# More unread products between TensorE's first steps, in banks chosen by another rule

## The chip, the cores and the metric

The kernel runs on one core of a Trainium2 chip. The metric is device time in microseconds (us) of one execution. Three executions of the kernel before gave 292.33, 293.51 and 296.66 us; a fourth, profiled one gave 292.35 us, and every duration below comes from that one.

## What is computed

Attention with an exponential feature map and no softmax matrix, and behind it a feed-forward layer with a maximum over three products:

```
def phi(x):
    proj = einsum('bhsd,df->bhsf', x, w_phi)
    proj = proj - max(abs(proj), axis=-1)
    return concatenate([exp(proj), exp(-proj)], axis=-1)
q_p, k_p = phi(q), phi(k)
kv  = einsum('bhsf,bhsd->bhfd', k_p, v)
z   = sum(k_p, axis=2)
att = einsum('bhsf,bhfd->bhsd', q_p, kv) / (einsum('bhsf,bhf->bhs', q_p, z) + 1e-6)
x   = att, heads side by side            # 4608 x 512
h   = maximum(maximum(x @ w1, x @ w2), x @ w3)
out = h @ w_out                          # 4608 x 512
```

There are 8 batches of 8 heads, 576 tokens a head, head size 64, 128 features, and a hidden width of 768. Inputs and output are float32; TensorE multiplies bfloat16.

## The kernel before

**Units and chunks.** The attention is cut into 16 units of four heads of one batch, two units a batch. The feed-forward layer is cut into chunks of 512 tokens, one a batch and one for the tokens that are left over. Both are described as nodes: a node is one step on one engine, with its instructions, the buffers it uses and the nodes it depends on.

**One unit** (`attention`, L428) loads q, k and v; casts q and k to bfloat16; transposes them (`tps`, L491, on TensorE for the first four units, else by DMA) and copies the result to `qkT` (L494, VectorE); projects them with w_phi (`psq`, `psk`, L528 and L533); takes maxima on VectorE (L552, `mqp` for q, `mk` for k) and exponentials of the k projection on ScalarE (`Ek`, L546); scales v on GpSimd by an exponential of the k maxima (`em`, L584, and `vab`, L588); computes the transposed q projection less its maximum (`psm`, L615 and L618 in the first four units) and its exponentials on ScalarE (`Eq`, L626); then forms kv (`kvps`, L642), the numerator and denominator (`psn`, L660) and their quotient (`x_sb`, L667). Among the steps of the first two units stand steps that prepare weights: transposes `pwT` (L800) and products `pm` (L814).

**Order.** Nothing is scheduled while the kernel runs. A table of words (`PLAN`, L97) gives every node an engine, a planned start in us, and the number of each buffer slot that it takes. A node `13T1@5.9` is node 13 on TensorE (T), with slot 1, at 5.9 us; D, A, G and S stand for VectorE, ScalarE, GpSimd and SyncE. `plan` (L250) reads the table. Each engine runs its instructions in the order of planned starts and waits on semaphores for what it needs.

**Banks.** TensorE writes into eight banks of 2 KB a partition. Each result takes a bank by number. When a new tile is made in a bank, its first writer waits for the last user of the tile that was there, and that includes an earlier write of TensorE itself.

**Unread products.** `fill` (L268) goes through TensorE's nodes in planned order. Where the plan leaves a gap between the end of one and the start of the next, it puts in products that nobody reads: 128x512, of a constant tile `idle`, made at L846 (tile `idler`). They go in at steps of 0.43 us up to 4.6 us of the plan (`SLOW`) and of 0.26 us from there on; gaps of up to 0.35 us are left alone up to `WARM` = 28 us of the plan, and of up to 0.5 us behind it. For each it looks for a bank in which no result lies around that time: the planned use of every result in it has ended by 0.1 us before, or begins over 0.6 us after. A product that is put in is itself recorded in `spans`, as a use of 0.5 us.

The names that the prediction speaks of are the products (L846), the first transposes (L491), the projections (L528, L533), `psm` (L615, L618), `pwT` (L800) and `kvps` (L642). In the diff the changed loop is L281 to L287.

Of the kernel before, what the change touches and what calls it, by code (L numbers as in the profile page):

```python
# [41 lines left out]
X_PE = 6  # L42
SUBT = 4
HALVES = 1
WARM = 28.0
SLOW = 4.6
JOIN = 2
MOVE = 5
# [219 lines left out]
def fill(order, spare, make, ready):  # L268

    pool = spare.pool  # L270
    spans, todo, free = {}, [(n.start, n.fn) for n in order], 0.0
    for n in order:
        for b in n.bufs:
            if b.pool is pool and b is not spare:
                x = spans.setdefault(id(b), [b.index, n.start, n.end])
                x[1], x[2] = min(x[1], n.start), max(x[2], n.end)
    for n in order:
        if n.eng != "PE":
            continue
        gap, t = n.start - free, max(free + 0.1, ready)  # L280
        while gap > (0.35 if t < WARM else 0.5) and t < n.start - 0.2:  # L281
            for i in range(len(pool.last)):
                if all(x[0] != i or x[2] < t - 0.1 or x[1] > t + 0.6 for x in spans.values()):
                    todo.append((t, make(i)))
                    spans[t] = [i, t, t + 0.5]
                    break
            t += 0.26 if t > SLOW else 0.43  # L287
        free = n.start + n.costs["PE"]
    return [fn for _, fn in sorted(todo, key=lambda x: x[0])]

# [2 lines left out]
def kernel(  # L293
# [554 lines left out]
    for fn in fill(order, spare, product, n_idle.end):  # L848
        fn()
# [28 lines left out]
```

## Time and profile before

| what | value |
|---|---|
| median of three executions | 293.51 us (292.33 to 296.66) |
| the profiled execution | 292.35 us |
| its span in the trace | 290.6 us |
| TensorE matmul busy | 279.4 us, 96% |
| VectorE, ScalarE, GpSimd busy | 215.9, 189.9, 117.4 us |
| unread products (L846) | 23, from 1.0 to 16.8 us |
| their length, shortest, median, longest | 0.376, 0.634, 0.634 us |
| last work of TensorE ends | 285.9 us |

How to read the views: busy times are what an engine spent in its instructions. A matmul's end is modelled and matmuls overlap, so a TensorE that reads as busy is not at its peak, and the start times tell more than the busy time. In a timeline, columns are start, length, engine, line, operation, written tile and what it was made from, shape and count; in square brackets stands the idle time ahead of it and what ended it. A line with a count is a run of instructions that follow each other, and its length reaches from the first start to the last end. The chain of waits follows the work that ended last back through what released each step.

### The profile page before, as it was taken

The page shows a single profiled execution, that of the slowest core. Times are in us where ns is not written, and L with a number is a line of the kernel's source. Part 1 is how long each engine was busy: PE and PEld are TensorE (multiplying, and loading weights), DVE is VectorE, ACT ScalarE, POOL GpSimd, SP SyncE. Part 2 cuts the span into 40 slices and gives each one's busy share as a digit, 9 for nine tenths or more (in the row PEclk, how much of TensorE's full clock was granted, in tenths as well). Part 3 has the DMA queues.
Part 4 walks back from the last instruction along what each step waited for, and adds up shares of the span by engine and source line. Part 5 has one row for each costly group of instructions (what it writes and reads, how often), then busy time and mean ns, then how long its engine had stood idle before and what let it go on. Part 6 is the DMA issues. An engine that isn't in the chain of part 4 may idle for free.

```text
span 290.6 us, 8659 instructions
## 1 busy us (share of the span) xinstructions
PE 279.4 (96%) x3602; PEld 158.7 (55%) x3641; DVE 215.9 (74%) x457; ACT 189.9 (65%) x438; POOL 117.4 (40%) x101
## 2 busy tenths in 40 slices
PE   8878999999999999999999999999999999999993
PEld 3556685646645585564466556545555564444442
DVE  2987999998876899768989959898796583242360
ACT  1599798977988899799669797566858631120101
POOL 8086886276093751552780519107064300000000
PEclk9999999999999999999999999999999999999999
DMA  7999988997967799796995779658534523500605
GB/s 191 208 201 181 218 249 271 230 335 178 356 132 258 221 189 279 165 287 130 298 182 106 173 235 206 138 126 174 102 107 95 112 21 72 126 18 2 144 18 128
DMA packets 63051, 49.87 MB, mean 172 GB/s; under 512 B 43556, under 2 KB 48036, under 8 KB 63012
## 3 DMA queue, kind: packets, MB, share of 16 engines
q1 hardware_dynamic: 58644, 44.04, 61.2%
q0 software_dynamic: 4288, 5.21, 11.0%
q8 instruction: 28, 0.46, 0.6%
q14 instruction: 11, 0.09, 0.1%
q10 hardware_dynamic: 80, 0.07, 0.1%
HBM read 34.67 MB, written 9.44 MB: 152 GB/s over the span
## 4 chain that ended last, share of the span: by engine, by line
PE 86%; DVE 6%; ACT 4%; DMA 2%; issue 1%; SPq 0%; ACTq 0%
PE ups L713 30%; PE ops L746 16%; PE ops L741 11%; PE kvps L642 7%; PE psn L660 6%; PE psq L533 5%; PE psm L613 4%; DVE mqp L552 2%; DMA wphi_f<-in_w_phi_dram 2%; DVE mk L552 2%; ACT Ek L546 2%; PE tps L491 1%; PE pxT L680 1%; PE psm L618 1%; PE psq L528 1%
## 5 line engine op out<-in xcount | busy, mean ns | idle before, releaser
L588 POOL TENSOR_TENSOR vab<-v_raw,em 128x1152 bf16<-128x1152 f32 (+1 forms) x36 | 68.2, 1907 | 88.7 <-ACT em L584 67.7
L713 PE MATMUL ups<-xT,w_bf 128*128 128x512 bf16 x411 | 100.7, 379 | 1.1
L546 ACT ACTIVATE Ek<-psk 128x512 bf16<-128x512 f32 x128 | 70.5, 607 | 23.7 <-PE psk L533 17.0
L626 ACT ACTIVATE Eq<-psm 128x512 bf16<-128x512 f32 (+1 forms) x160 | 79.2, 586 | 7.9 <-PE psm L613 6.2
L713 PEld LDWEIGHTS <-w_bf 128*128 128x128 bf16 x432 | 40.3, 98 | 44.1 <-DVE x_sb L667 0.2
L746 PE MATMUL ops<-wout_bf,hT 128*128 128x512 bf16 (+1 forms) x219 | 50.7, 373 | 0.3
L552 DVE TENSOR_REDUCE mqp<-psq 128x4 bf16<-128x512 f32 (+1 forms) x80 | 47.7, 631 | 2.0 <-PE psk L533 1.0
L719 DVE TENSOR_TENSOR hT<-hT,ups 128x512 bf16<-128x512 bf16 x54 | 35.9, 683 | 14.2 <-ACT hT L721 6.8
L552 DVE TENSOR_REDUCE mk<-psk 128x4 f32<-128x512 f32 x64 | 42.5, 681 | 1.7 <-ACT Ek L546 1.2
L746 PEld LDWEIGHTS <-hT 128*128 128x128 bf16 x222 | 21.3, 98 | 22.8 <-DVE hT L719 0.2
L721 ACT ACTIVATE hT<-ups 128x512 bf16<-128x512 f32 x28 | 16.4, 613 | 26.2 <-PE ups L713 26.1
L667 DVE TENSOR_TENSOR x_sb<-psn,rden 128x320 bf16<-128x320 f32 x64 | 31.5, 492 | 2.2
L660 PEld LDWEIGHTS <-Eq 128*128 128x128 bf16 x640 | 24.5, 97 | 6.5 <-issue 0.3
L754 DVE COPY osb<-ops 128x512 f32<-128x512 f32 (+1 forms) x19 | 12.6, 674 | 18.9 <-PE ops L746 18.9
L660 PE MATMUL psn<-kv_sb,Eq 128*128 128x65 bf16 x640 | 26.3, 193 | 0.1
L723 DVE TENSOR_SCALAR hT<-ups 128x512 bf16<-128x512 f32 x26 | 17.5, 686 | 11.4 <-PE ups L713 11.1
L754 ACT COPY osb<-ops 128x512 f32<-128x512 f32 (+1 forms) x18 | 10.3, 575 | 23.7 <-DMA out_dram<-osb 9.6
L741 PE MATMUL ops<-xT 128*128 128x512 bf16 x86 | 24.1, 380 | 0.5
L642 PEld LDWEIGHTS <-Ek 64*128 64x128 bf16 x1152 | 18.4, 94 | 5.7 <-issue 2.8
L642 PE MATMUL kvps<-vab,Ek 64*128 64x65 bf16 x1152 | 20.5, 190 | 0.9 <-POOL vab L588 0.5
L533 PE MATMUL psq<-w,qkT 64*128 64x128 bf16 x256 | 20.4, 217 | 0.4 <-DVE qkT L494 0.4
L533 PEld LDWEIGHTS <-qkT 64*128 64x128 bf16 x512 | 14.5, 94 | 10.7 <-issue 7.7
(72 smaller groups left out, 277.8 us busy)
## 6 DMA issues: line engine op xcount, KB each, us to landing
v_raw<-in_v_dram SPq DMA_DIRECT2D x16, 576.0 KB, 4.6
out_dram<-osb SPq DMA_DIRECT2D x70, 128.0 KB, 2.4
k_raw<-in_k_dram SPq DMA_DIRECT2D x12, 576.0 KB, 4.9
q_raw<-in_q_dram SPq DMA_DIRECT2D x12, 576.0 KB, 6.1
w_bf<-in_moe_w_dram POOLq DMA_DIRECT2D x3, 768.0 KB, 10.0
qk_bf<-in_q_dram POOLq DMA_DIRECT2D x3, 288.0 KB, 10.6
qk_bf<-in_k_dram POOLq DMA_DIRECT2D x3, 288.0 KB, 11.1
wout_bf<-in_moe_w_out_dram POOLq DMA_DIRECT2D x1, 768.0 KB, 9.5
```

The lines of the kernel that those rows point to most:

```text
L533: nc.tensor.matmul(ps()[:, i, :], lhsT=cols[r, :], rhs=w2[r, c, :], start=True, stop=True)
L546: nc.scalar.activation(Ek[s]()[:, tiles_of(t0, n), :], of(1), EXP, scale=1.0 - 2.0 * s)
L552: nc.vector.tensor_reduce((mq, mk)[c]()[:, tiles_of(t0, n)], of(c), AXX, ALU.max, apply_absolute_value=True)
L588: (nc.vector if n_.eng == "DVE" else nc.gpsimd).tensor_tensor(vab()[:, g, t0:t1, 0:D], vb()[:, t0:t1, :], em()[:, g, t0:t1].unsqueeze(2).t ...
L626: nc.scalar.activation(Eqb()[s][:, cols], psm()[:, 0:w], EXP, scale=1.0 - 2.0 * s)
L642: nc.tensor.matmul(kvps[ab]()[:, t // NT, g, :], lhsT=Ek[g]()[r, t, :], rhs=vab()[r, g, t, :], start=(t + g == 0), stop=(t == UT - 1 and g ...
L660: nc.tensor.matmul(psn()[:, c, :], lhsT=Eqb()[g][:, t0:t0 + P], rhs=kv()[:, pr, ab, g, :], start=(g == 0), stop=(g == 1))
L667: nc.vector.tensor_tensor(x_sb()[:, pr, :, ab, :], psn()[:, :, 0:D], rden().to_broadcast([P, 5, D]), ALU.mult)
L713: nc.tensor.matmul(ups(), lhsT=w_bf[i + 1][:, ct, j * P:(j + 1) * P], rhs=tokens_of(ct), start=(ct == 0), stop=(ct == CT - 1))
L719: nc.vector.tensor_tensor(hT()[:, j, :], hT()[:, j, :], ups(), ALU.max)
L741: nc.tensor.matmul(ops_()[:, 0:width], lhsT=tile_of(ct, tt), rhs=line_w[c_i > MOVE][:, ct, cols], start=(ct == 0), stop=False)
L746: nc.tensor.matmul(ops_()[:, 0:width], lhsT=hT()[:, j, tt * P:(tt + 1) * P], rhs=wout_bf[:, j, cols], start=False, stop=(j == JT - 1))
```

## The change

`WARM` goes from 28 to 34, and the loop of `fill` is changed in these ways:

- up to `WARM`, gaps from 0.25 us on get products (before: 0.35);
- products go in up to 0.1 us ahead of the waiting step (before: 0.2), 0.22 us apart (before: 0.26);
- where the gap is over 0.6 us, up to two more go in right ahead of the waiting step (`late`);
- a bank may also be taken if its next planned use begins with the waiting step or later (before: over 0.6 us after the product);
- a product is no longer recorded in `spans`, so a bank that one product took is free for the next, and the search, which goes from bank 0 up, takes the first that fits each time.

The table of the order is the same, and so are all other steps. In the built program there are 49 products where there were 23. 38 of them wait for TensorE's own count of the product directly ahead of them; before, the nearest such wait was for the last but one.

```diff
-WARM = 28.0
+WARM = 34.0
...
         gap, t = n.start - free, max(free + 0.1, ready)
-        while gap > (0.35 if t < WARM else 0.5) and t < n.start - 0.2:
+
+        late = 2 if gap > 0.6 and t < WARM else 0
+        while gap > (0.25 if t < WARM else 0.5) and (t < n.start - 0.1 or late):
+            if t >= n.start - 0.1:
+                t, late = n.start - 0.02 * late, late - 1
             for i in range(len(pool.last)):
-                if all(x[0] != i or x[2] < t - 0.1 or x[1] > t + 0.6 for x in spans.values()):
+                if all(x[0] != i or x[2] < t - 0.1 or x[1] >= n.start for x in spans.values()):
                     todo.append((t, make(i)))
-                    spans[t] = [i, t, t + 0.5]
                     break
-            t += 0.26 if t > SLOW else 0.43
+            t += 0.22 if t > SLOW else 0.43
         free = n.start + n.costs["PE"]
```

## The prediction

> **What bounds the kernel now.** I read the page first: TensorE is the busiest engine, and nearly full from the fourth slice on.
>
> ```profile
> span 290.6 us, 8659 instructions
> PE 279.4 (96%) x3602; PEld 158.7 (55%) x3641; DVE 215.9 (74%) x457; ACT 189.9 (65%) x438; POOL 117.4 (40%) x101
> PE   8878999999999999999999999999999999999993
> ```
>
> Then the busy time by stage (columns: length, then PE, PEld, DVE, ACT, POOL busy with their instructions, granted clock, DMA share, GB/s).
>
> ```profile
> 0.00:7.00 7.00, 5.96 (x19) 2.09 (x21) 2.13 (x12) 1.28 (x1) 6.15 (x14) 1.00 0.77 186
> 7.00:12.50 5.50, 5.36 (x80) 2.93 (x75) 4.60 (x11) 2.67 (x6) 0.00 (x0) 1.00 1.11 215
> 12.50:17.00 4.50, 3.60 (x57) 2.56 (x55) 4.37 (x9) 4.01 (x14) 1.47 (x2) 1.00 1.21 206
> 17.00:21.60 4.60, 3.34 (x72) 2.18 (x72) 3.86 (x8) 4.60 (x12) 4.58 (x6) 1.00 0.94 200
> 28.00:60.00 32.00, 31.63 (x550) 20.71 (x552) 30.03 (x67) 27.47 (x63) 22.41 (x15) 1.00 0.99 237
> 60.00:200.00 140.00, 138.78 (x1938) 80.00 (x1960) 118.31 (x252) 110.77 (x256) 65.71 (x49) 1.00 0.83 208
> ```
>
> From 28 us on TensorE idles 1% of the time (0.37 of 32, 1.22 of 140 us). So a delay that stands at 28 us has almost nothing to be made good with and moves the end one for one; a gain there would too. All 23 unread products lie before 17 us. What they do is in the timeline:
>
> ```profile
> 1.04 0.61 PE L846 MATMUL idler<-idle 128*128 128x512 bf16 x1 [1.04 <-DVE idle L414]
> 1.04 5.73 PE L846 MATMUL idler<-idle 128*128 128x512 bf16 x13 [1.04 <-DVE idle L414]
> 6.14 0.63 PE L846 MATMUL idler<-idle 128*128 128x512 bf16 x1
> 6.70 0.80 PE L491 MATMUL tps<-ident,qk_bf 128*64 128x128 bf16 x16
> 7.43 1.04 PE L846 MATMUL idler<-idle 128*128 128x512 bf16 x4
> 8.40 1.06 PE L491 MATMUL tps<-ident,qk_bf 128*64 128x128 bf16 x20
> 9.57 0.22 PE L533 MATMUL psk<-w,qkT 64*128 64x128 bf16 x1
> 9.83 0.60 ACT L546 ACTIVATE Ek<-psk 128x512 bf16<-128x512 f32 x1 [7.82 <-PE psk L533]
> 11.75 0.88 PE L846 MATMUL idler<-idle 128*128 128x512 bf16 x3
> 12.46 0.27 PE L615 MATMUL psm<-qkT,w 128*128 128x256 bf16 x1
> 17.06 1.20 PE L491 MATMUL tps<-ident,qk_bf 128*64 128x128 bf16 x36
> 21.08 0.20 PE L642 MATMUL kvps<-vab,Ek 64*128 64x65 bf16 x1 [0.47 <-POOL vab L588]
> 21.68 0.20 PE L642 MATMUL kvps<-vab,Ek 64*128 64x65 bf16 x2 [0.40 <-DVE mqp L552]
> ```
>
> Three prices come from here. (a) Spacing of products that do not wait: (6.14 - 1.04) / 12 = 0.425 us in the first 6 us, and (1.04 - 0.38) / 3 = 0.22 us from 7.43 on: TensorE runs at half speed until somewhere between 6.14 and 7.43 (the granted clock reads 1.00 throughout and does not show it; the durations do). (b) Length of one: 0.61 to 0.63 us slow, 0.38 to 0.39 fast. (c) From a product's end to the start of what waits for it: the ScalarE Ek at 9.83 waits for the projection whose last psk product is the line above it, 9.57 + 0.22 = 9.79, so 0.04 us; the DVE cast that ends at 8.72 lets TensorE go on at 8.76, again 0.04.
>
> And the chain of waits: DVE, not TensorE, is last in most of 10 to 21 us, behind TensorE's transposes and projections:
>
> ```profile
> 10.10 1.78 DVE mqp L552 x3
> 12.91 1.53 DVE mk L552 x3
> 17.74 1.49 DVE qkT L494 x3
> 20.42 1.21 DVE mqp L552 x2
> 21.68 1.25 PE kvps L642 x71
> ```
>
> **The change, part by part.** The other engines' instructions stand in the same order. On TensorE the built program has 49 products for 23: before the first transposes 16 (13), before the second 7 (4), before the third projection 2 (1), before the fifth 5 (1), before the first psm 7 (3), the first pwT 1 (0), unit 1's transposes 4 (1), its first two projections 2 and 1 (0), before kvps 4 (0). WARM = 34 adds none behind 21.2 of the plan.
>
> What decides is not the count. Before, the record in `spans` made neighbouring products take different banks, and one waited at the nearest for the last but one. Without it the search takes the first bank that fits each time, so whole groups write bank 0. In the built program 38 of the 49 wait on TensorE's own count for the product directly ahead. So they go one by one: length plus 0.04, that is 0.66 us slow (0.425 now) and 0.43 fast (0.22 now). No row of before shows such a wait at work. Its bounds: no dearer than streaming (0.425, 0.22), and length plus 0.04. I take the upper end: the built waits leave no way to start earlier than the end of the product ahead, and 12.46 fits, 0.05 behind the end of the product it waits for.
>
> Arrivals on TensorE, in us, if it turns fast at 7.1 as now (case A). First transposes: 9 products slow, 7 fast, from 1.04: 9 x 0.66 + 6 x 0.435 + 0.22 = 8.8, at 9.8 (now 6.70, where their DMA had just landed, so nothing was lost). Second transposes: + 0.45 + 6 x 0.435 + 0.22, at 13.1 (8.40; the cast they need is there at 8.72). First projection 13.65 (9.39). Third, behind two products: 14.75 (10.26); the DVE copy it needs ends about 14.5. Fifth, + 0.45 + 4 x 0.435 + 0.22: 17.2 (11.13). First psm, + 0.25 + 6 x 0.435 + 0.22: 20.3 (12.46); the DVE maxima that it reads end about 18.3, so DVE no longer sets the pace. Up to unit 1's transposes 3.4 us of own work and 4 products in two banks (1.3 us): 25.0 (17.06). Its projections 26.9 (18.49), one of which waits for a product in its own bank. kvps: the bank-4 products wait for the same DVE maximum as kvps itself, then take 4 x 0.435 = 1.7 us right on the path: 31.5 (21.68). GpSimd's vab, behind ScalarE's em, is late by 7 only and hides. The sum is +9.8 us; up to 0.9 of it may come back where TensorE sat for 0.9 us at 26.1.
>
> Does it turn fast at 7.1? In the trace TensorE had streamed without a gap from 1.04 and was still slow at 6.14, 5.1 us later. Changed, it streams 0.425 of each 0.66 us, 65%, and no stretch without gaps is over 2 us before the psm steps. The nearest row is the stretch that was 100% used and needed over 5 us, so I take it as not turning fast in these products. Then slow: first transposes 11.4, second 16.7 (0.85 for 16 transposes, 7 x 0.66), first projection 17.75, third 19.7. From 16.7 on, transposes, projections and two products follow closely, and I let it turn fast there, at about 20 (case B). Fifth projection 22.3, first psm 25.4, from there as in A: kvps at 36.6, +14.9. Sum against the profiled execution's own 292.35 us, less 0.5 for the gap: 306.7. The median of the runs shown is 293.51, 1.2 above it; I state 306.5.
>
> The Trainium skill ("TensorE: Matmul & The Clock Gate", part 1, on the HAM clock gate) says that the half clock ends after one busy window of some 3.4 us that runs free of the kernel, and returns after an idle one. The trace agrees with the first, if its window of 100% is what is needed. For the second, the longest gap of TensorE after 7.43 is 0.91 us and no product behind it is slow again: by that rule there is no closed gate here for more products to open, which speaks against any gain. If waiting products count as busy, the rule gives case A.
>
> **Rivals.** (1) Case A, 292.35 + 9.8 - 0.5 = 301.6, with turning fast up to a window later 303. For it: each product is under way 0.62 of 0.66 us. Against it: 5.1 us of gapless products were not enough.
> (2) Slow until the psm and pwT steps: 3 to 4 us more than B, 310. For it: transposes and projections come in stretches of 2 us only.
> (3) Not slower: the wait on the product ahead is over before that product's modelled end, so spacing stays 0.425 and 0.22. Then only 26 more products: first psm about 2 us later, kvps about 3, partly in waits on DVE: 295.5. It decides at a fast spacing of about 0.31 us (3 us at 0.22, 9.8 at 0.435, and 2% is 5.9). Against it: Ek's start shows that the end is counted.
> (4) Faster: executions such as the 296.66 hold a stretch at half speed that more products prevent: 291 to 292. Nothing in the profile shows one.
>
> **How the numbers follow.** B 0.45, A 0.30, (2) 0.10, (3) 0.13, (4) 0.02. 2% is about what a measurement of this kernel can tell from no change, here 299.4. Slower by over 2%: B, (2) and nearly all of A, 0.84; within: (3) and a little of A, 0.14; faster 0.02. The range leaves out (3), (4) and the far end of (2): from A with a microsecond more made good, 299.5, to (2) with 2 us more, 312. B's own is 304 to 309.
>
> **What would show it.** In the changed profile: products of a group 0.66, later 0.43 us apart; TensorE fully busy to 20 us by the page, yet the first psm at 25 (A: 20) and kvps near 36 (A: 31); DVE and ScalarE idle behind TensorE between 10 and 25; from there the same steps as before, moved as a block. The forecast is wrong if products are 0.22 apart with the same waits (rival 3), or if TensorE makes up the delay behind 28 us. The length of the second group's products (0.38 or 0.63) tells A from B.

## The result, and the profile after

The changed kernel takes 306.22 us (305.07 to 307.46, six runs) against 293.53 us: 1.043 times as long, 95% interval 1.037 to 1.049. Its profiled execution took 305.07 us, with a span of 303.3 us, 12.7 more than before. Medians and ranges here take in every run; the ratios, here and below, leave out the runs that the record marks as slow. In line numbers, 3 is to be added to those of before, and up to 6 in the experiments.

The page of the changed kernel: the time of each engine, slices, and the chain that ended last by line.

```profile
span 303.3 us, 8710 instructions
PE 292.8 (97%) x3628; PEld 160.9 (53%) x3667; DVE 216.1 (71%) x457; ACT 190.5 (63%) x438; POOL 117.4 (39%) x101
PE   7999999999999999999999999999999999999993
PE ups L716 28%; PE ops L749 15%; PE ops L744 10%; PE idler L849 7%; PE kvps L645 6%; PE psn L663 6%; PE psq L536 5%; PE psm L616 4%; PE tps L494 2%; ACT Ek L549 1%; PE psm L618 1%; PE psm L621 1%; DVE mk L555 1%; DVE mqp L555 1%; PE pxT L683 1%
```

TensorE reads busier than before (97% for 96%) in a kernel that is slower. VectorE's and ScalarE's busy times have stayed (216.1 for 215.9, 190.5 for 189.9 us), so no work is dearer. What has grown is the share of `idler` in the chain that sets the end: 7%, some 21 us. Before, one product stood on that chain:

```profile
16.76 0.38 PE idler L846
```

VectorE's share of that chain fell from 6% to 3%.

The stages, in the columns of before:

```profile
7.00:12.50 5.50, 5.16 (x24) 1.48 (x23) 0.97 (x4) 0.00 (x0) 0.00 (x0) 1.00 1.13 220
12.50:17.00 4.50, 4.16 (x17) 0.97 (x17) 0.48 (x1) 0.00 (x0) 0.00 (x0) 1.00 1.21 207
72.00:212.00 140.00, 138.78 (x1939) 79.93 (x1960) 118.27 (x252) 110.99 (x257) 65.70 (x49) 1.00 0.85 207
```

Between 7 and 17 us VectorE works 1.45 us where it worked some 9, and ScalarE not at all, while TensorE counts as busy with 41 instructions. The stage from 72 to 212, which is that from 60 to 200 set 12 us back, has the same 138.78 us of TensorE. The timeline says what those 41 are:

```profile
1.04 10.21 PE L849 MATMUL idler<-idle 128*128 128x512 bf16 x16 [1.04 <-DVE idle L417]
11.18 1.06 PE L494 MATMUL tps<-ident,qk_bf 128*64 128x128 bf16 x16
12.18 4.45 PE L849 MATMUL idler<-idle 128*128 128x512 bf16 x7
16.56 1.28 PE L494 MATMUL tps<-ident,qk_bf 128*64 128x128 bf16 x20
22.00 2.98 PE L849 MATMUL idler<-idle 128*128 128x512 bf16 x7
24.82 0.27 PE L618 MATMUL psm<-qkT,w 128*128 128x256 bf16 x1
33.70 1.67 PE L849 MATMUL idler<-idle 128*128 128x512 bf16 x4 [0.32 <-DVE mqp L555]
35.43 1.27 PE L645 MATMUL kvps<-vab,Ek 64*128 64x65 bf16 x72
```

The first 16 stand (10.21 - 0.58) / 15 = 0.64 us apart (0.425 before), the seven at 12.18 also 0.64, and those from 18 us on 0.43 (0.22): in the group at 22.00, (2.98 - 0.38) / 6. No idle time is shown in these groups, because the modelled end of one and the start of the next lie 0.05 us apart. The wait shows in the spacing alone.

Matching the 457 VectorE instructions of both traces one by one gives the lateness along the kernel: 3.7 and 7.8 us at the first two copies to qkT, 8.4 at the first maxima and 9.9 at those that follow, 12.6 at unit 1's maxima, 13.4 at unit 2's first copy, then 12.4 to 12.7 from 28 us of the kernel before on, and 12.69 from 51 us to the end of the work. The 0.7 that VectorE made good goes with the stop of TensorE at 26.1 us, which the trace of before has and this one has not; TensorE itself stood 13.8 us late ahead of that stop and 12.7 behind it. The rest moved as a block.

### The profile page after: what moved, and what is told of

It reads as the page before. It is cut to its first block, busy times and chain, and to the rows that moved or that the text cites. A ratio compares the mean times of both kernels' runs of the same rounds, so it can differ in the third digit from the quotient of the medians.

```text
span 303.3 us, 8710 instructions
## 1 busy us (share of the span) xinstructions
PE 292.8 (97%) x3628; PEld 160.9 (53%) x3667; DVE 216.1 (71%) x457; ACT 190.5 (63%) x438; POOL 117.4 (39%) x101
## 3 DMA queue, kind: packets, MB, share of 16 engines
q0 software_dynamic: 4288, 5.21, 10.4%
## 4 chain that ended last, share of the span: by engine, by line
PE 91%; DVE 3%; ACT 3%; issue 1%; ACTq 0%
PE ups L716 28%; PE ops L749 15%; PE ops L744 10%; PE idler L849 7%; PE kvps L645 6%; PE psn L663 6%; PE psq L536 5%; PE psm L616 4%; PE tps L494 2%; ACT Ek L549 1%; PE psm L618 1%; PE psm L621 1%; DVE mk L555 1%; DVE mqp L555 1%; PE pxT L683 1%
## 5 line engine op out<-in xcount | busy, mean ns | idle before, releaser
L724 ACT ACTIVATE hT<-ups 128x512 bf16<-128x512 f32 x28 | 16.4, 613 | 26.2 <-PE ups L716 26.1
L849 PE MATMUL idler<-idle 128*128 128x512 bf16 x49 | 23.2, 476 | 3.5 <-DVE idle L417 1.0
L757 DVE COPY osb<-ops 128x512 f32<-128x512 f32 (+1 forms) x19 | 12.6, 674 | 18.9 <-PE ops L749 18.9
L726 DVE TENSOR_SCALAR hT<-ups 128x512 bf16<-128x512 f32 x26 | 17.5, 686 | 11.4 <-PE ups L716 11.1
L536 PEld LDWEIGHTS <-qkT 64*128 64x128 bf16 x512 | 14.6, 94 | 11.2 <-issue 8.0
```

What stands on the lines that cost most here:

```text
L849: nc.tensor.matmul(idler, lhsT=idle, rhs=idle.unsqueeze(1).to_broadcast([P, 4, P]), start=True, stop=True)
```

## The experiments

Theory W: what costs is that each product waits for the one ahead, and that TensorE, used too thinly by such a chain, stays at half speed. Rival C: their number costs, in whatever bank. Rival P: the ones right ahead of a waiting step cost. Ratios are to the kernel before, run on the same chip.

**The same 49 products, in banks taken in turn**

```diff
+    used = {}
...
-            for i in range(len(pool.last)):
-                if all(x[0] != i or x[2] < t - 0.1 or x[1] >= n.start for x in spans.values()):
-                    todo.append((t, make(i)))
-                    break
+            fit = [i for i in range(len(pool.last))
+                   if all(x[0] != i or x[2] < t - 0.1 or x[1] >= n.start for x in spans.values())]
+            if fit:
+                i = min(fit, key=lambda i: used.get(i, -1.0))
+                used[i] = t
+                todo.append((t, make(i)))
```

> All 49 products of the changed kernel at the same places, but each takes the fitting bank that was used longest ago, so that almost none waits for the product directly ahead. Theory W (the waits on the product ahead, and the half speed that they prolong, make the 12.7 us): products 0.425 and 0.22 us apart, full speed by about 7 us, first psm near 14.5 us, kvps near 25, time about 296, ratio to before about 1.01. Rival C (the products' own number is what costs, whatever bank they are in): stays near 306, ratio 1.04. Rival P (it is the products put right ahead of the waiting step): near 303 or more, ratio 1.03, since those are all still there.

Measured: 294.98 us, 1.006 (1.002 to 1.010). Its timeline:

```profile
1.04 5.93 PE L852 MATMUL idler<-idle 128*128 128x512 bf16 x16 [1.04 <-DVE idle L420]
7.48 1.68 PE L852 MATMUL idler<-idle 128*128 128x512 bf16 x7
12.93 1.90 PE L852 MATMUL idler<-idle 128*128 128x512 bf16 x7
25.00 1.27 PE L648 MATMUL kvps<-vab,Ek 64*128 64x65 bf16 x72
```

As many products, in the same places, cost 2.5 us of span instead of 12.7. The group of seven takes 1.68 for 4.45 us. Rivals C and P fall as the main cause; together they keep at most the 2.5 us (kvps at 25.0, expected near 25).

Rotation takes away two things at once: the wait, and the writing of one bank twice in a row. The trace of the kernel before tells them apart. Its `ups` products (L713, 128x512 too) write one bank four times in a row, adding up, and the program puts no wait on TensorE's own count between them. Its chain of waits shows 44 of them:

```profile
269.04 9.50 PE ups L713 x44
```

They stand 9.50 / 44 = 0.216 us apart, like products that stream. So one bank again is not by itself what spaces products out; the wait is what is left.

**Rotation in the first group alone, and in all groups but the first**

```diff
-                i = min(fit, key=lambda i: used.get(i, -1.0))
+                i = min(fit, key=lambda i: used.get(i, -1.0)) if n.start < 6.0 else fit[0]
```

> The changed kernel, with the banks rotated in the first group of 16 alone; the other 33 stand as in the changed kernel, most of them waiting for the one ahead. Theory W with the clock as a part of it: 16 gapless products bring full speed at about 7 us, the first transposes come at 7.9, the waits of the other groups cost 0.43 for 0.22 us, kvps at about 29.5; time about 300, ratio 1.024. If half speed alone made the loss (the waits at full speed cost nothing that counts): 296, ratio 1.01. If the waits alone made it and not the speed: only the 3 to 4 us of the first group come back, 302 to 303, ratio 1.03.

Measured: 297.94 us, 1.017 (1.011 to 1.023); span 296.1. The counterpart has `n.start > 6.0` in that line.

> The counterpart of the rotated first group: in the changed kernel's 16 first products each waits for the one ahead, the 33 others rotate their banks. Theory W: first transposes at 11.2 us as in the changed kernel, then a stretch used over three quarters (transposes, then 7 products without gaps), so full speed at 13 to 16 us, first psm near 21, kvps near 31; time 302, ratio 1.027. If half speed and the waits of the later groups were what cost, and the first group's late end did not: 297, ratio 1.01.

Measured: 300.68 us, 1.025 (1.019 to 1.031); span 299.4, full speed at 15.3 us, first psm at 21.2. The views show first the kernel with the first group rotated, then its counterpart:

```profile
1.04 5.52 PE L852 MATMUL idler<-idle 128*128 128x512 bf16 x16 [1.04 <-DVE idle L420]
7.06 2.98 PE L852 MATMUL idler<-idle 128*128 128x512 bf16 x7
28.32 1.27 PE L648 MATMUL kvps<-vab,Ek 64*128 64x65 bf16 x72
```

```profile
12.18 3.17 PE L852 MATMUL idler<-idle 128*128 128x512 bf16 x7
31.30 1.27 PE L648 MATMUL kvps<-vab,Ek 64*128 64x65 bf16 x72
```

The spans add up: all rotated +2.5 over before; the waits of the first group, with the half speed that they prolong, 299.4 - 293.1 = 6.3; the waits of the other 33, at full speed, 296.1 - 293.1 = 3.0. That makes 11.8 of 12.7. The rest, 0.9, is no more than single executions of one kernel differ by; it may fall where both are present, on the seven products at 12.18, which then run at half speed throughout (4.45 us for 2.98 or 3.17). The ratios add up less far, to 0.6 + 1.9 + 1.1 = 3.6 of 4.3%, each to about half a per cent. What the waits of the first group cost by themselves, and what the half speed, was not taken apart. For the first of the two, 300 was expected and 298 measured: full speed came at 4.9 us, not at 7, within the first group.

**The kernel before, without the record in `spans`**

```diff
                     todo.append((t, make(i)))
-                    spans[t] = [i, t, t + 0.5]
                     break
```

> The kernel before with one line taken out, the one that records a product as a user of its bank; 25 products for 23, nearly all in bank 0, each waiting for the one ahead. Theory W: 0.64 us apart and slow, first transposes at about 9.3 us (6.7 before), first psm about 5 us later than before, full speed not before 10 us; time about 298.5, ratio 1.017. Rival C: 2 products more, so at most 1 us, ratio 1.00. Rival P: no products near the waiting steps are added, ratio 1.00.

Measured: 299.78 us, 1.020 (1.009 to 1.031); span of the profiled execution 295.8. First transposes at 9.26, first psm at 17.44, 5.0 later than before, and the first kvps at 25.1, 4.0 later.

```profile
1.04 8.29 PE L845 MATMUL idler<-idle 128*128 128x512 bf16 x13 [1.04 <-DVE idle L413]
```

The one line does this without the new thresholds, without products right ahead of the waiting step, and with 2 products more than before. It is the part of the change that costs: alone 2.0%, where the 49 products in rotated banks cost 0.6%. The rest of the 4.3% takes both, 38 waits in place of the 19 that this kernel's built program has.

**The changed kernel without the four products ahead of kvps**

```diff
         late = 2 if gap > 0.6 and t < WARM else 0
+        if n.kind == "K":
+            gap = late = 0
```

> The changed kernel without the four products ahead of the first kvps, which wait for the same VectorE maximum as kvps and then stand one by one on its path. Theory W: kvps starts 4 x 0.43 = 1.7 us sooner behind that maximum, time 304.5, ratio 1.037. If kvps waits for something else by then (GpSimd's vab): under 0.5 us, 306, ratio 1.042.

Measured: 305.15 us, 1.040 (1.033 to 1.047), which does not settle it. The trace does, up to kvps: from the first psm to kvps' run of 71 it takes 32.94 - 23.45 = 9.5 us, for 35.43 - 24.82 = 10.6.

```profile
32.34 0.20 PE L647 MATMUL kvps<-vab,Ek 64*128 64x65 bf16 x1 [0.33 <-DVE mqp L557]
32.94 1.25 PE L647 MATMUL kvps<-vab,Ek 64*128 64x65 bf16 x71 [0.40 <-DVE mqp L557]
55.21 0.30 PE L647 MATMUL kvps<-vab,Ek 64*128 64x65 bf16 x8 [1.06 <-issue]
```

The gain is 1.1, not 1.7: kvps writes two banks and waits for a second VectorE maximum, and the products had covered part of that. Its span is still 303.2 us, no shorter, though its kvps ran 2.5 us sooner than the changed kernel's (1.4 of it because full speed came sooner). TensorE stops for 0.69 us up to 36.9 and for 1.06 up to 55.2, for nothing that the profile shows, and the changed kernel's own trace has neither stop; the rest went in smaller pieces by 57 us. So in this trace the gain at kvps does not reach the end. The ratios, 1.040 for 1.043, put what reached it at 0.8 us, which is within the noise.

**What the products of before are worth, and how thinly they may stand**

Three kernels, each the kernel before with one thing changed: the first 13 products alone; none; and the first 13 in banks 0, 0, 2, 2 in turn, so that every second one waits.

```diff
-        while gap > (0.35 if t < WARM else 0.5) and t < n.start - 0.2:
+        while gap > (0.35 if t < WARM else 0.5) and t < n.start - 0.2 and n.start < 6.0:
...
+        while False:
...
+    spans_first = []
...
+            if n.start < 6.0:
+                todo.append((t, make((0, 0, 2, 2)[len(spans_first) % 4])))
+                spans_first.append(t)
+                t += 0.26 if t > SLOW else 0.43
+                continue
```

> The kernel before with its first 13 products alone; the other 10, between 7.4 and 16.8 us, are left out. If they held nothing up and kept nothing up: 293.5, ratio 1.00. If they delay the steps behind them: the product at 16.76 us, which waits for ScalarE and stands on the chain of waits, goes, and the second unit's transposes come 0.3 to 0.4 us earlier, ratio 0.998 to 1.00. If they kept TensorE at full speed: some matmuls behind 10 us at half speed, up to 3 us more, ratio 1.01.

Measured: 293.02 us, 1.001 (0.997 to 1.004).

> The kernel before without any unread product. If they only fill time: 293.5, ratio 1.00, first transposes still at 6.7 us when their load lands. If they are what brings full speed: half speed until the steps stand close, at 13 to 17 us or later, first psm at 13 to 14, kvps 2 to 4 us late, time 296 to 297.5, ratio 1.01.

Measured: 295.15 us, 1.007 (1.003 to 1.012). The time came out near what was expected, the steps did not: full speed came at 11.05 us and went again from 14.47 to 17.88, the first psm came at 12.08 (12.46 before) and the first kvps at 22.18 (21.08 before), 1.1 late and not 2 to 4. The profiled execution took 298.28 us, the longest of the ten, so its later part does not tell where the 0.7% lies.

> The kernel before with its first 13 products in banks 0, 0, 2, 2 and so on, so that every second one waits for the one ahead: 0.64 and 0.43 us apart in turn, TensorE used 80% of the time where one wait for each uses 67%. If a window of about three quarters use is enough for full speed: full speed between 4.5 and 8 us, first transposes at 7.4 to 7.9, time 293.5 to 295, ratio 1.00 to 1.005. If only products without gaps give it: half speed to 10 us or later, 296 to 298, ratio 1.01 to 1.015.

Measured: 294.70 us, 1.003 (0.999 to 1.008); full speed at 7.3 us, first transposes at 7.70.

So the products of before are worth 0.7% together, and the last ten of them no time that can be measured. They do have an effect, and it goes both ways. Without these ten the first psm comes at 11.46 us, 1.0 sooner than before: they hold it up. But the trace of that kernel then shows half speed again from 13.17 to 16.58 us (the column behind POOL's is the granted clock), and its first kvps is 0.3 late, at 21.38.

```profile
9.75:13.17 3.42, 2.35 (x30) 1.19 (x30) 3.42 (x7) 3.42 (x9) 0.00 (x0) 1.00 1.18 210
13.17:16.58 3.41, 2.97 (x27) 2.43 (x28) 2.73 (x7) 2.35 (x9) 1.42 (x2) 0.50 1.21 208
```

No version here is faster than the kernel before by more than its runs differ.

## Why the prediction was right, point by point

| step | predicted (B) | measured |
|---|---|---|
| spacing of products, slow and fast | 0.66, 0.43 us | 0.64, 0.43 us |
| first, second transposes | 11.4, 16.7 us | 11.18, 16.56 us |
| first, third, fifth projection | 17.75, 19.7, 22.3 us | 17.77, 19.07, 21.67 us |
| full speed | about 20 us | 17.7 us |
| first psm | 25.4 us | 24.82 us |
| kvps | 36.6 us | 35.43 us |
| made good behind kvps | 0.5 (up to 0.9) us | 1.1 us on TensorE |
| end | 306.7 us by the sum, 306.5 stated | 305.07 us profiled, 306.22 us median |

**The waits** were read off the built order, and their price, length plus 0.04 us, was taken from other waits. The traces confirm it at both speeds, to 0.02 us. Rival (3) is excluded for this kernel, and its 295.5 us for streaming products is what the rotated kernel measured (294.98).

**Full speed** came behind the first two groups, as case B had it, for a reason that was only partly right and with some luck. The step "the stretch that was 100% used and needed over 5 us" took gapless use to be needed. The pairs, with a wait at every second product, turned fast at 7.3 us; the rotated first groups, without gaps, at 4.9 and 5.75, that is 3.9 and 4.7 us after their start at 1.04. So gapless use was not needed, nor five microseconds of it. The shares of windows of 3.41 us, in the section on the hardware, account for most of it: in the trace of before one such window ran from 0.25 us and held products from 1.04 on alone. The moment also differs between executions of the same steps: the kernel without the products ahead of kvps, the same up to there, had full speed at 14.0, one window and 0.3 us sooner, and its first psm 1.4 us sooner. That 17.7 came as near to 20 as it did is in part luck.

**The sum at kvps** was 1.2 us too high. Half of it stands at the third projection (19.7 for 19.07) and stays to the first psm: full speed came 2.3 us sooner than put. The other half lies between the first psm and kvps, for which 11.2 us were reckoned and 10.6 measured; the products ahead of kvps are the term, 1.7 us where the experiment found 1.1.

**The stated time** fits better than its sum. The sum starts from an execution of 292.35 us and gives 306.7; the profiled execution of the changed kernel, which it compares with, took 305.07, 1.6 less: 1.2 from kvps, and some 0.5 because TensorE made good 1.1 us behind kvps (13.75 late there, 12.7 at the end) and not 0.5. The prediction notes that the median lies 1.2 above that execution, but does not add it. With it the sum would have said 307.9 for a median measured at 306.22. That 306.5 came within 0.3 of the median is luck; added up, the steps missed by 1.6.

**That the delay moves the end one for one** held to 0.02 us from 51 us of the kernel before to its end. A gain did so too in the kernels with rotated banks: against the changed kernel their kvps came 4.1, 7.1 and 10.4 us sooner and their spans were 3.9, 7.2 and 10.2 us shorter. In the kernel without the products ahead of kvps it did not, for the stops named there.

**The rule weighed against the change** held in its conclusion: the products of the change brought no gain, and the kernel with ten products fewer than before is as fast. The argument had a hole. That no gap was long enough to lose full speed was read from a trace in which the products filled the gaps; taken out, full speed was lost for 3.41 us without an idle window.

## What to carry to other kernels

A product that nobody reads is not free of its destination: two in a row to one bank, each as a tile of its own, run end to start instead of start to start, because the second is made to wait for the first: 0.64 for 0.425 us at half speed and 0.43 for 0.22 at full. Look in the built order for waits of an engine on its own count, and in the trace at start-to-start times; a busier TensorE can be a slower one. A chain meant to bring up TensorE's speed has to use more than some three quarters of its time, as far as these traces tell, or it prolongs what it is there to end.

## What the runs showed of the hardware

The granted clock in the traces changes at moments that lie 3.41 us apart, or a multiple of it, within one trace. So windows of that length are counted here back and forth from a change. For each window the share is reckoned in which some product of TensorE, read or unread, streams (512 columns take 0.427 us at half speed and 0.216 at full, and fewer columns in proportion, from the starts on record; an estimate). It goes with the changes of speed, but for a narrow band.

| window | use | then |
|---|---|---|
| changed kernel, 4.05, 7.46, 10.87 | 0.63, 0.68, 0.74 | half speed stays |
| changed kernel, 14.29 | 0.76 | full speed |
| before, 0.25 and 3.66 | 0.77 and 0.96 | stays, then full speed |
| before without the record, 5.95 and 9.36 | 0.66 and 0.74 | stays, then full speed |
| pairs, 3.93 | 0.77 | full speed |
| changed, without the products ahead of kvps, 10.55 | 0.75 | full speed |
| first 13 alone, 6.34 and 9.75 | 0.51 and 0.38 | full speed stays, then half |
| without any unread product, 7.64 and 11.05 | 0.77 and 0.35 | full speed, then half |

So from 0.74 to 0.77 both were seen: five windows brought full speed and two did not, and nothing here tells them apart. In the first 60 us of all ten traces, 0.72 and less never brought it and 0.86 and more always did; a fall to 0.38 or less lost it (three windows), and 0.49 did not. The Trainium skill ("TensorE: Matmul & The Clock Gate", part 1) has the window of about 3.4 us, which these traces agree with (3.41), and asks for an idle window before half speed returns; here one used 38% was enough.

TensorE also stops now and then for nothing that the profile shows: for 0.91 us from 26.1 in the kernel before, 1.31 from 26.9 with the first 13 products alone, 1.20 from 28.1 and 2.43 from 46.1 without any, 1.06 from 54.2 in the kernel without the products ahead of kvps. Behind the stop of 2.43 us the granted clock reads half from 48.60 to 52.01; the window ahead of that had a share of 0.20. What causes the stops was not found.
